# Where three weight scales are read, and where one scan sum is taken, in a fused attention and gated-GLU kernel

## The chip, the cores and the metric

One Trainium2 chip, one core. The time is the device time of one execution in microseconds; the median of three runs is given. A profile is one further execution, recorded by the hardware profiler, with a time of its own.

## The reference

Everything is bf16 outside, with x of 2048 rows and 640 columns. B is a gated unit with 1536 hidden features. A is attention with 32 heads of 192, in which every query sees the last 512 cached keys (Sk // 4 of 2048).

```python
xn = layernorm(x)
q = (xn @ wq) split into 32 heads of 192
k, v = k_cache[:, :, Sk - W:], v_cache[:, :, Sk - W:]        # W = 512
s = softmax(q @ k.T * 192 ** -0.5) @ v, heads joined, @ wo
g = silu((sigmoid(xn @ w_gate) * (xn @ w_up)) @ w_down)
out = x + s * g
```

## The kernel before

The work has three stages. The first (lines 404 to 541) normalizes x and computes the hidden features of B. The second, about 124 to 643 us, is attention in 16 runs. The third multiplies by wo and w_down and joins the parts. The order of all instructions is written out by hand: each engine takes its own in the order in which the program issues them, and waits in place where an operand is not ready.

**The runs.** A run r is a pair (pi, g): half pi of the queries (1024 rows), group g of four heads. Even runs have pi = 0, odd ones pi = 1, and g is r // 2. A run has a score phase of 16 steps, k = 0 to 15, and then a value phase of 8 products, k = 0 to 7.

- A step of the score phase is `stage_s` (six pairs of matmuls into a pair of PSUM banks, line 663, then one exp on ACT, line 667) and then `phase_s`, which issues whatever else belongs to that step. Banks 4 to 7 take turns, so the scores of step k wait for the exp of step k - 2.
- A product of the value phase is `stage_pv`: 16 matmuls (line 677), a reciprocal and a scaling on VectorE (lines 683 and 684), and after every second one a DMA transpose of the result on SP's queue (line 690). The transposed result is stored later, also by SP (`store_o`, line 697).

**Queries of the next run.** In the same score steps, eleven query slots compute the next run's queries (`query_slots`; `q_after` puts them at k = 1, 2, 3, 4, 5, two at 6, then 8, 10, 12, 14). They use seven products where eight would be plain, in a half-and-half scheme on fp16 sums of the weights. Their matmuls are line 569; VectorE copies a product out of PSUM (line 590) and adds it to another (line 607). The slots share banks 0 to 3 with the value products that follow: the second value product needs the banks that slot 10, at k = 14, frees with its last add.

**Scales.** The fp16 sums need weights scaled by a power of two. There is one scale for two groups, four in all, each from the absolute sums of five chunks of wq:

- `scan_load(i, buf)` loads chunk i by SP; `scan_abs(i)` (line 202) takes the absolute sum per partition on ACT. Chunks 5n to 5n + 4 belong to scale n. The tables `scans_s` and `scans_pv` say at which (r, k) of the score phase or of the value phase a sum is taken.
- `set_scan(n)` calls `set_scale`: VectorE takes the maximum of the five columns, cuts it to a power of two, spreads it over a tile mx_b, and SP transposes it by DMA into mx_row (line 213), so that each partition then holds all 128 values. Table `sets` gives the place.
- `set_scale2` reads the row: a maximum over mx_row (line 216), a product (line 217) and a reciprocal (line 218), all on VectorE. Table `sets2` gives the place. This is what "reading a scale" means here.

The first scale is set and read in the first stage. The other three are set at (1, 1), (4, 1) and (9, 1). Scale n serves groups 2n and 2n + 1: `weights(g, c)` scales raw weights with it on ACT in the value phases, two runs or so ahead, and `scale_k` (line 170) multiplies K with its inverse, at k = 12 of an even run (14 in run 2) and at k = 7 of an odd one. K comes into the tile kraw by two DMAs on SP (`load_k`, line 161), for an even run at k = 2 and at k = 12 or 14.

The places in `phase_s` that matter, in their order within a step:

```python
for j in q_after.get(k, ()) if q_list else ():
    q_list[j]()
...
if pi == 0 and g + 1 < NG:
    if k == 2:
        load_k((g + 1, 0))
    elif k == (14 if g == 1 else 12):
        scale_k((g + 1, 0))
        load_k((g + 1, 1))
...
if (r, k) in scans_s:
    scan_abs(scans_s[r, k])
...
if (r, k) in sets2:
    n = sets2[r, k]
    set_scale2(mx, w_ups[n], w_downs[n])
```

Of the kernel before, what the change touches and what calls it, by code (L numbers as in the profile page):

```python
# [17 lines left out]
def kernel(  # L18
# [177 lines left out]
    def scan_load(i, buf):  # L196
        scan_t[i] = buf[:, 0:NSC]
        n, c = divmod(i, NCD)
        nc.sync.dma_start(scan_t[i], wq_n[:, c, n * NSC:(n + 1) * NSC])
# [536 lines left out]
    for n, k in enumerate((0, 1, 7, 2, 3, 8, 4, 5, 9, 6, 10)):  # L736
# [5 lines left out]
        elif n == 4:  # L742
            for i in range(6):
                scan_load(NCD + i, scan_bufs[i])
    scans_s = {(0, 4): 10, (0, 10): 11}
    scans_pv = {(0, 0): 5, (0, 1): 6, (0, 2): 7, (0, 4): 8, (0, 6): 9, (1, 7): 12, (2, 7): 13, (3, 7): 14}
    scans_pv.update({(4 + n, 7): 15 + n for n in range(NCD)})
    scans_load = {(0, 6): (11, 5), (1, 4): (12, 4), (2, 4): (13, 5), (3, 4): (14, 4)}
    scans_load.update({(4 + n, 4): (15 + n, 5 - n % 2) for n in range(NCD)})
    sets = {(1, 1): 1, (4, 1): 2, (9, 1): 3}  # L750
    sets2 = {(1, 8): 1, (4, 9): 2, (9, 8): 3}
    scale_s = {0: 2, 3: 3, 15: 4}
    q_after = {1: (0,), 2: (1,), 3: (2,), 4: (3,), 5: (4,), 6: (5, 6), 8: (7,), 10: (8,), 12: (9,), 14: (10,)}

# [444 lines left out]
```

## Time and profile before

| | before |
|---|---|
| median of three runs | 877.39 us (876.77 to 877.61) |
| profiled execution, its own time | 877.93 us |
| its span | 876.1 us |
| TensorE busy | 865.4 us, 7557 matmuls |
| VectorE busy | 674.9 us |
| ACT busy | 628.5 us |
| GpSimd busy | 234.8 us |
| mean granted TensorE clock | 0.998 |

The span runs from the first to the last recorded instruction. An engine counts as busy while one of its instructions runs. The granted clock is the share of full speed that TensorE was given. A wait is put down to the instruction that ended last before the waiting one began. In the views below, PE is TensorE, DVE is VectorE, ACT is ScalarE, POOL is GpSimd and SP is the engine whose queue issues most DMAs.

### The profile page before, as it was taken

What the parts mean: (1) busy time and instruction counts of PE and PEld (TensorE: products, weight loads), DVE (VectorE), ACT (ScalarE), POOL (GpSimd) and SP (SyncE); (2) the same over time, 40 slices, a digit from 0 to 9 for tenths busy, and PEclk for the clock granted to TensorE, in tenths of its full rate; (3) what the DMA queues carried; (4) which work ended last, traced back from release to release, by engine and by line L of the source; (5) the groups of instructions that cost most, each with busy time, mean ns of one, the idle gap of its engine ahead of it and who ended that gap; (6) DMA issues with size and microseconds to landing.
All of it is one profiled execution on the core that took longest, in us unless ns stands there. A gap on an engine that the chain in (4) does not pass through costs nothing.

```text
span 876.1 us, 19052 instructions
## 1 busy us (share of the span) xinstructions
PE 865.4 (99%) x7557; PEld 570.9 (65%) x7557; DVE 674.9 (77%) x1148; ACT 628.5 (72%) x783; POOL 234.8 (27%) x320
## 2 busy tenths in 40 slices
PE   9999999999998999999999999999999999999998
PEld 5444446576676775775775775775777777777775
DVE  6586767877875776776877877888788788979997
ACT  4766568799797889889889688648556566866662
POOL 0085076062360443443442442300000111000000
PEclk9999999999999999999999999999999999999999
DMA  9895983978998899899989968899696977776641
GB/s 281 185 249 109 243 240 83 262 101 234 227 165 218 156 209 237 181 205 241 169 168 225 170 120 206 206 220 261 140 277 184 302 240 221 235 251 219 224 136 37
DMA packets 258873, 175.98 MB, mean 201 GB/s; under 512 B 162976, under 2 KB 241440, under 8 KB 258784
## 3 DMA queue, kind: packets, MB, share of 16 engines
q1 hardware_dynamic: 253248, 157.26, 72.4%
q0 software_dynamic: 5536, 17.50, 10.4%
q8 instruction: 59, 0.97, 0.5%
q14 instruction: 30, 0.25, 0.1%
HBM read 101.71 MB, written 36.70 MB: 158 GB/s over the span
## 4 chain that ended last, share of the span: by engine, by line
PE 94%; ACT 2%; DMA 1%; DVE 1%; SPq 1%; issue 0%; DVEq 0%; ACTq 0%
PE ps_all L1007 25%; PE ps_all L677 20%; PE ps_all L569 19%; PE ps_all L663 18%; PE ps_all L484 11%; ACT E L667 1%; PE ps_all L387 1%; ACT arm L722 1%; DMA mx_row<-mx_b 0%; DMA kraw<-in_A_k_cache_dram 0%; SPq L697 0%; DMA x_sb<-in_A_x_dram 0%; DVE arm L991 0%; DVE arm L1062 0%; DVE arm L1060 0%
## 5 line engine op out<-in xcount | busy, mean ns | idle before, releaser
L667 ACT ACTIVATE E<-ps_all 128x1024 bf16<-128x1024 f32 x256 | 251.6, 1024 | 97.9 <-PE ps_all L663 97.7
L663 PE MATMUL ps_all<-qT,kT 64*128 64x512 bf16 x1536 | 199.9, 378 | 0.9 <-ACT E L667 0.8
L677 PEld LDWEIGHTS <-E 128*128 128x128 bf16 x2048 | 169.7, 98 | 8.3 <-issue 8.3
L677 PE MATMUL ps_all<-v_sb,E 128*128 128x193 bf16 x2048 | 174.1, 247 | 0.1
L607 DVE TENSOR_TENSOR qT<-ps_all,qp 128x512 bf16<-128x512 f32 x174 | 115.6, 687 | 47.8 <-PE ps_all L569 38.3
L1007 PEld LDWEIGHTS <-mid 128*128 128x128 f16 x1236 | 120.3, 98 | 46.0
L663 PEld LDWEIGHTS <-kT 64*128 64x128 bf16 x1536 | 86.6, 94 | 79.6 <-issue 6.1
L590 DVE COPY qp<-ps_all 128x512 f32<-128x512 f32 x150 | 100.5, 687 | 43.8 <-PE ps_all L569 43.6
L684 DVE TENSOR_TENSOR o_st<-ps_all,rden 128x768 bf16<-128x768 f32 x128 | 122.5, 957 | 4.7 <-DVE rden L683 0.3
L569 PE MATMUL ps_all<-mid 64*128 64x512 f16 (+1 forms) x840 | 106.8, 377 | 3.5 <-DVE qp L590 3.5
L569 PE MATMUL ps_all<-mid,arm 64*128 64x512 f16 (+1 forms) x840 | 105.6, 376 | 0.0
L569 PEld LDWEIGHTS <-mid 64*128 64x128 f16 x840 | 50.3, 94 | 46.4 <-issue 5.5
L569 PEld LDWEIGHTS <-arm 64*128 64x128 f16 x840 | 47.1, 94 | 44.5 <-issue 0.5
L1007 PE MATMUL ps_all<-arm,mid 128*128 128x320 f16 x480 | 70.4, 299 | 0.0
L808 ACT ACTIVATE mid<-mid,w_sc 128x1536 f16<-128x1536 bf16 (+1 forms) x43 | 61.4, 1451 | 0.0
L240 ACT ACTIVATE mid<-mid,w_sc 128x1536 f16<-128x1536 bf16 x37 | 58.1, 1571 | 1.1 <-DVE w_sc L218 0.7
L1007 PE MATMUL ps_all<-op,mid 128*128 128x320 f16 (+1 forms) x408 | 58.1, 295 | 0.0
L490 DVE TENSOR_TENSOR hT_sb<-ps_all,sig_sb 128x512 bf16<-128x512 f32 x48 | 32.8, 686 | 28.3 <-PE ps_all L484 20.7
L489 ACT ACTIVATE sig_sb<-ps_all 128x512 bf16<-128x512 f32 x48 | 28.4, 596 | 35.3 <-PE ps_all L484 33.9
L258 POOL TENSOR_TENSOR arm<-mid 128x384 f16<-128x384 f16 x20 | 18.2, 909 | 119.9 <-ACT mid L240 118.9
L258 POOL TENSOR_TENSOR mid<-mid 128x384 f16<-128x384 f16 x20 | 18.2, 909 | 118.9 <-ACT mid L240 117.9
L1007 PE MATMUL ps_all<-mid 128*128 128x320 f16 x348 | 49.9, 299 | 0.0
(183 smaller groups left out, 1094.1 us busy)
## 6 DMA issues: line engine op xcount, KB each, us to landing
oT_d<-oT SPq DMA_DIRECT2D x64, 384.0 KB, 5.0
mid<-oT_d SPq DMA_DIRECT2D x46, 384.0 KB, 4.1
mid<-in_A_wq_dram POOLq DMA_DIRECT2D x64, 192.0 KB, 7.1
arm<-in_A_wo_dram SPq DMA_DIRECT2D x16, 480.0 KB, 6.3
h_d<-hT_sb SPq DMA_DIRECT2D x16, 384.0 KB, 4.5
kraw<-in_A_k_cache_dram SPq DMA_DIRECT2D x32, 192.0 KB, 3.4
v_sb<-in_A_v_cache_dram SPq DMA_DIRECT2D x32, 192.0 KB, 5.8
arm<-in_A_wq_dram SPq DMA_DIRECT2D x15, 384.0 KB, 4.7
```

The lines of the kernel that those rows point to most:

```text
L240: nc.scalar.activation(raw.bitcast(F16), raw, AF.Copy, scale=w_ups[g // 2])
L258: tt(TB, part_w(g, c, a, 1, 1), part_w(g, c, a, 0, 1), ALU.subtract)
L484: nc.tensor.matmul(gu[:, i, :], lhsT=w[:, c, f * P:(f + 1) * P], rhs=xnT[s][:, c, :], start=(c == 0), stop=(c == NCD - 1),)
L569: nc.tensor.matmul(ps_all[:, b, :], lhsT=w(r, c), rhs=x[r, c, :], start=(first and k == 0), stop=(k == len(cs) - 1), skip_group_check=True,)
L590: nc.vector.tensor_copy(dst, part(b))
L607: nc.vector.tensor_tensor(q_out(i, u, pp), part(b), t, ALU.add)
L663: nc.tensor.matmul(ps[:, b, :], lhsT=kT[h, c * PC + j, :], rhs=qT_t[r][i, j][h, pp, :], start=(j == 0), stop=(j == PC - 1),)
L667: nc.scalar.activation(E_t[r, i, pp][:, c, :, :], ps, AF.Exp, scale=scale_qk)
L677: nc.tensor.matmul(o_ps[:, q // 2, q % 2, 0:DH + 1], lhsT=E[:, c, h, q * P:(q + 1) * P], rhs=vt[:, c, 0:DH + 1], start=(c == 0), stop=(c = ...
L684: nc.vector.tensor_tensor(o_st[:, :, h * DH:(h + 1) * DH].rearrange("p (b i) d -> p b i d", b=2), o_ps[:, :, :, 0:DH], rden[:].to_broadcas ...
L808: eng.activation(t, t.bitcast(BF16), AF.Copy, scale=up)
L1007: nc.tensor.matmul(ps_all[:, b, d0:d1], lhsT=a[:, c, :], rhs=w[:, c, d0:d1], start=(start and c == 0), stop=(c == nk - 1), skip_group_chec ...
```

## The change

Three entries of `sets2` move: the read of scale 1 from step 8 to step 12 of run 1, that of scale 2 from step 9 of run 4 to step 0 of run 5, that of scale 3 from step 8 to step 12 of run 9. The places of `set_scan` stay. The absolute sum of chunk 11 moves from step 10 of run 0 to the end of its value phase, behind the last product. The load of that chunk stays at step 6. No instruction is added or taken away, and the orders on TensorE, GpSimd and SP stay as they are.

```diff
-    scans_s = {(0, 4): 10, (0, 10): 11}
-    scans_pv = {(0, 0): 5, (0, 1): 6, (0, 2): 7, (0, 4): 8, (0, 6): 9, (1, 7): 12, (2, 7): 13, (3, 7): 14}
+    scans_s = {(0, 4): 10}
+    scans_pv = {(0, 0): 5, (0, 1): 6, (0, 2): 7, (0, 4): 8, (0, 6): 9, (0, 7): 11, (1, 7): 12, (2, 7): 13, (3, 7): 14}
     scans_pv.update({(4 + n, 7): 15 + n for n in range(NCD)})
     scans_load = {(0, 6): (11, 5), (1, 4): (12, 4), (2, 4): (13, 5), (3, 4): (14, 4)}
...
     sets = {(1, 1): 1, (4, 1): 2, (9, 1): 3}
-    sets2 = {(1, 8): 1, (4, 9): 2, (9, 8): 3}
+    sets2 = {(1, 12): 1, (5, 0): 2, (9, 12): 3}
```

## The prediction

> **What bounds the kernel now.** I read the busy shares first, then PE's waits, then the 16 attention runs one against another, then each odd run's chain and queues.
>
> ```profile
> PE 865.4 (99%) x7557; PEld 570.9 (65%) x7557; DVE 674.9 (77%) x1148; ACT 628.5 (72%) x783; POOL 234.8 (27%) x320
> PE ps_all L569 <- DVE qp L590: 3.5, 1, 3.5
> PE ps_all L663 <- ACT E L667: 0.8, 1, 0.8
> ```
>
> The first line is the page's busy time, the other two are from PE's waits (total, times, longest). TensorE works 99% of the 876.1 us, so only what stops or slows it counts. Two stops lie in the part that the diff touches: one of 3.5 us behind a VectorE copy, one of 0.8 us behind an exp.
>
> Next I cut the runs at their first score matmul and asked for busy time by stretch. Columns: the stretch, its length, then each engine's busy time, granted clock, DMA share, GB/s.
>
> ```profile
> 124.14:157.93 33.79, 32.90 (x331) 22.53 (x328) 26.42 (x43) 26.79 (x32) 21.90 (x31) 1.00 0.58 128
> 157.93:190.61 32.68, 32.68 (x332) 20.52 (x333) 25.07 (x47) 28.44 (x36) 7.60 (x10) 1.00 0.83 200
> ...
> 256.04:294.18 38.14, 34.65 (x331) 26.14 (x333) 25.54 (x47) 29.67 (x33) 15.85 (x21) 0.96 0.80 167
> 294.18:326.89 32.71, 32.71 (x332) 21.90 (x333) 24.07 (x40) 28.43 (x36) 10.55 (x14) 1.00 1.03 210
> 326.89:359.82 32.93, 32.87 (x332) 21.98 (x333) 24.33 (x40) 29.55 (x33) 16.02 (x22) 1.00 0.92 208
> ```
>
> These are runs 0, 1, 4, 5 and 6. An undisturbed run takes 32.71 us. Run 4 takes 38.14 (5.43 too many), run 0 takes 33.79 (1.08 too many), run 6 takes 32.93 (0.22 too many). Run 1, which holds a scale read too, loses nothing; nor does run 9 (32.71).
>
> **Run 4.** From the chain of waits there (start, length, what):
>
> ```profile
> 270.12 2.09 SPq L697
> ...
> 272.27 4.29 DMA mx_row<-mx_b
> ...
> 276.58 0.30 DVE w_sc L216
> ...
> 277.25 0.60 DVE qp L590
> 277.86 0.04 issue
> 277.90 1.26 PE ps_all L569 x10
> ```
>
> VectorE had the row ready for its transpose at about 261, but SP's queue stood in the stores of line 697 and issued the transposing DMA at 272.27. The read at step 9 stands in front of a copy (line 590) that TensorE needs, so all wait until 276.56. By the starts of equal matmuls, run 6 goes on 18.10 us after its beginning, run 4 at 277.90 - 256.04 = 21.86: 3.76 us lost. Then TensorE is slow (one-microsecond stretches of PE: length, busy, clock, DMA share, GB/s):
>
> ```profile
> 277.90:278.90 1.00, 1.00 (x10) 1.00 0.02 6
> 278.90:279.90 1.00, 1.00 (x10) 0.60 0.00 0
> 279.90:280.90 1.00, 1.00 (x8) 0.50 0.00 0
> 280.90:281.90 1.00, 1.00 (x8) 0.50 0.00 0
> 281.90:282.90 1.00, 1.00 (x10) 0.70 0.53 155
> ```
>
> Lost to the clock: 0.40 + 0.50 + 0.50 + 0.30 = 1.70 us. 3.76 + 1.70 = 5.46, the 5.43 of the run.
>
> **Part 1: the read of run 4 moves to step 0 of run 5.** The stall goes, as the row has landed some 12 us before the new place. What is late next? In the same run at step 12 VectorE scales K from kraw, whose loads stand on SP right behind the transpose (SP issues them from 273.63). Today the stall hides that. Without it VectorE is there as in run 6, which shows this wait:
>
> ```profile
> 344.21 4.23 DMA kraw<-in_A_k_cache_dram
> ...
> 348.46 0.42 DVE k_sb L170
> ```
>
> Run 6's second half of kraw landed at 348.44, which is 21.55 us into the run; the late scaling pushed back the last query add (end at 350.29), for which the second value product waited: 0.22 us. For run 4, SP's semaphore row on the same load line ends its wait at 277.6, and the landing times of this window are at most 3.4 us after issues at 273.63 and about 274.2; so kraw is there at 277.6, 21.56 us into the run. That is run 6 to a hundredth. I take run 6's loss, 0.22. Bounds: nothing, if it lands 0.3 us sooner; above, the slowest landing of line 161 in the traced runs, 5.9 us (run 2), would make it 280.1, so 2.5 us more, at one microsecond of TensorE for each. Run 4: 38.14 - 32.93 = 5.21 saved.
>
> At its new place the read takes 0.78 us of VectorE (run 1's own: from 174.13 to the next copy at 174.91). In run 4's own first step VectorE idles 1.33 us before the first copy, and run 5 begins alike: cost 0. It issues no DMA; SP's and POOL's orders stay. Its readers (weight scaling in run 5's value phase, K in run 6) come 15 us later or more.
>
> **Part 2: the reads of runs 1 and 9 go from step 8 to step 12.** Neither waits today (transposes issued at 164.04 and 436.63, landed 5.0 and 2.9 us later, read at 174.13 and 441.47), so nothing is gained. Queued behind the new place is the copy of step 14 and its add, on which the second value product waits. In run 1 the adds ahead end at 178.64; with 0.78 the copy starts at 179.42 instead of 179.02, and its add ends 1.49 later at 180.91, 22.98 us into the run. Run 6's product was ready at 350.11, 23.22 us in. So 0.2 us of cover is left: cost 0, and if the cover were gone, 0.4 in each at most.
>
> **Part 3: the scan sum.** In run 0, ACT (start, length, what):
>
> ```profile
> 141.59 1.50 ACT L202 ACTIVATE arm<-arm 128x1536 bf16<-128x1536 bf16 x1
> 142.97 0.21 ACT L202 ACTIVATION_READ_ACCUMULATOR arm<-arm 128x1 f32 x1
> 143.06 3.88 ACT L667 ACTIVATE E<-ps_all 128x1024 bf16<-128x1024 f32 x4
> ```
>
> One absolute sum, 1.47 us to the next instruction, stands before four exps back to back, and the scores of two steps wait: 0.80 and 0.26 us of TensorE, 1.06 of the run's 1.08. Run 6 has the same steps without the sum and loses nothing there. At the new place, behind the last value product's entry in ACT's order, five sums end at 155.55 and the next exp waits for TensorE until 158.78: 3.23 us idle, of which a sixth takes 1.47 to 1.66. Its load was issued at 133.17, and its result is wanted only in run 4. Gain 1.08, bounds 0.80 (the named wait alone) and 1.11 (by the value phases' starts).
>
> **The sum.** The profiled execution took 877.93, with 1.83 outside the span of 876.1. Span: 876.1 - 5.21 - 1.08 = 869.8; that execution would take 871.64. The median of the three runs is 0.54 below it, so 877.39 - 6.29 = **871.1 us**. About 0.2%, 1.75 us, is what a measurement can tell here.
>
> [...] The row: 3.49 us without a matmul, then clock 0.50 to 0.60 for some 3 us. [...]
>
> **The rivals.**
>
> Slow clock only in the profiled execution. The gap is the same in every execution but its slow stretch may not be. Then the timed runs gain 3.76 - 0.22 + 1.08 = 4.62: 872.8. For it: the profiled time is above all three. Against: it is only 0.32 above the slowest, not 1.7. Chance 0.12. [...]
>
> A K load that comes later than I read. With the 5.9 us landing run 4 gives back 2.5 more: 873.6. For it: DMA share is 0.9 to 1.1 before the wait. Against: all DMAs up to 277 are issued as before. Chance 0.08.
>
> Slower: the stall is only passed on. Place: SP's queue in run 4. If its pause lets SP catch up, run 6's kraw would land 5.21 late, and TensorE would lose that plus 1.70 for the clock: 6.91 against 6.29, and with the 1.47 of a sum that still held back exps, 879.5. It decides from a slip of about 4.6 us. For it: SP issued run 4's transpose 11 us after it was ready. Against: in run 6 SP has issued all and waits from 345.7 to 348.9 although runs 5 and 6 had no pause, and run 8 repeats without loss (32.71). Chance 0.04.
>
> That the edit does nothing is out: the order of VectorE's instructions does move, and the 3.5 us name that read.
>
> **How the numbers follow.** Forecast 0.76, the rest as above. Low end: no kraw loss (870.9) less the runs' scatter of 0.6 and the 0.03 of part 3's upper bound: 870.2. High end: 873.6, the late K load, which takes in the clock rival. Below and above lie the slower case and part of the scatter. Faster by over 0.2%: 0.76 + 0.12 + 0.08, less 0.01 for what I have not seen, 0.95; slower 0.04; same 0.01.
>
> **What would show it.** Right: no PE wait on line 590; no DVE wait on mx_row after the first; run 4 at 32.9 us with clock 1.00 and a kraw wait of some 0.3; run 0 at 32.7; runs 1, 5 and 9 as before. Wrong: a kraw wait of over 1 us in run 4, a PE wait in the second value product of runs 1 or 9, a first exp of run 1 that waits for ACT, or a longer run 6.

## The result, and the profile after

The changed kernel takes 871.51 us (median of six runs, 871.22 to 872.36) against 877.08 us (875.24 to 877.77) for the kernel before in the same comparison: a ratio of 0.9941, interval 0.9928 to 0.9954. The forecast was 871.1, with a range from 870.2 to 873.6. The profiled execution took 872.36 with a span of 870.2, the slowest of the six; the other five have spans of 869.3 to 869.9.

The page's busy time:

```profile
PE 863.0 (99%) x7557; PEld 570.7 (66%) x7557; DVE 674.5 (78%) x1148; ACT 628.5 (72%) x783; POOL 234.3 (27%) x320
```

PE's waits (what waited for what: total, times, longest):

```profile
PE ps_all L377 <- DVE warm L371: 1.3, 1, 1.3
PE ps_all L677 <- DVE qT L607: 0.8, 1, 0.8
PE ps_all L387 <- ACT mid L402: 0.7, 2, 0.5
```

The wait of 3.5 us on a copy (line 590) and that of 0.8 us on an exp are gone. The first and the last line lie ahead of the attention runs. A new wait is there: a value product waits 0.8 us for the last query add. Runs 0, 4, 5, 6 and 8, each cut at its first score matmul (stretch, length, busy times, clock, DMA share, GB/s):

```profile
123.64:156.51 32.87, 32.87 (x334) 22.94 (x332) 26.55 (x44) 27.12 (x33) 22.02 (x32) 1.00 0.59 125
...
254.61:288.40 33.79, 32.94 (x331) 26.13 (x333) 25.02 (x44) 29.55 (x33) 16.74 (x23) 1.00 0.93 194
288.40:321.11 32.71, 32.71 (x331) 21.91 (x333) 24.56 (x43) 28.43 (x36) 9.60 (x14) 1.00 0.95 209
321.11:353.82 32.71, 32.71 (x331) 21.89 (x333) 24.16 (x40) 29.55 (x33) 15.79 (x22) 1.00 0.83 199
386.53:419.44 32.91, 32.88 (x331) 21.91 (x333) 24.34 (x40) 29.56 (x33) 15.98 (x22) 1.00 0.93 200
```

Run 4 fell from 38.14 to 33.79 and its clock from 0.96 went to 1.00. Run 0, which is 34.08 in the kernel before by this cut, is 32.87. Run 6 no longer loses its 0.22, and run 8 now loses 0.20. Run 4 is not at the 32.93 that was forecast, and its chain of waits says why:

```profile
272.30 0.97 SPq L213
...
273.94 3.05 DMA kraw<-in_A_k_cache_dram
...
277.02 0.42 DVE k_sb L170
277.44 0.61 DVE qp L590
...
278.15 0.70 DVE qT L607
...
278.89 9.49 PE ps_all L677 x112
```

This is the wait that the forecast named as next: K waits for kraw, behind it the copy, the add and then the second value product. Here and below, a time into run 4 is counted from its first score matmul in the timeline, 254.53 in this profile and 255.97 in the one before. In this execution SP issued the loads at 273.33, 18.8 us into the run (17.7 in the profile before), so VectorE waited 1.19 us and TensorE 0.85, as the last figures of these two rows of the timeline say:

```profile
276.52 0.93 DVE L170 TENSOR_SCALAR k_sb<-kraw,w_sc 128x768 bf16<-128x768 bf16 x2 [1.19 <-DMA kraw<-in_A_k_cache_dram]
...
278.89 9.49 PE L677 MATMUL ps_all<-v_sb,E 128*128 128x193 bf16 x112 [0.85 <-DVE qT L607]
```

### The profile page after: what moved, and what is told of

It is laid out like the page before. It is cut to its first block, busy times and chain, and to the rows that moved or that the text cites. A ratio compares the mean times of both kernels' runs of the same rounds, so it can differ in the third digit from the quotient of the medians.

```text
span 870.2 us, 19053 instructions
## 1 busy us (share of the span) xinstructions
PE 863.0 (99%) x7557; PEld 570.7 (66%) x7557; DVE 674.5 (78%) x1148; ACT 628.5 (72%) x783; POOL 234.3 (27%) x320
## 4 chain that ended last, share of the span: by engine, by line
PE 97%; DVE 1%; DMA 1%; SPq 0%; issue 0%; ACT 0%; DVEq 0%
PE ps_all L1007 26%; PE ps_all L569 21%; PE ps_all L677 20%; PE ps_all L663 19%; PE ps_all L484 11%; PE ps_all L387 1%; DMA kraw<-in_A_k_cache_dram 0%; DVE stats L349 0%; DVE arm L991 0%; DMA x_sb<-in_A_x_dram 0%; DVE arm L1062 0%; DVE arm L1060 0%; DVE qp L590 0%; DVE xn L364 0%; SPq L213 0%
## 5 line engine op out<-in xcount | busy, mean ns | idle before, releaser
L489 ACT ACTIVATE sig_sb<-ps_all 128x512 bf16<-128x512 f32 x48 | 28.4, 596 | 35.3 <-PE ps_all L484 33.8
```

## The experiments

Each was compared with the kernel before, run beside it. The medians of that kernel were 877.26, 877.77, 877.26 and 877.99 us for experiments 1 to 4, 5 to 8, 9, and 10 and 11.

### 1. The read of run 4 alone

```diff
-    sets2 = {(1, 8): 1, (4, 9): 2, (9, 8): 3}
+    sets2 = {(1, 8): 1, (5, 0): 2, (9, 8): 3}
```

> Only the read of scale 2 moves, from step 9 of run 4 to step 0 of run 5; scan sum 11 and the other two reads stay as before. The changed kernel's trace shows run 0 shorter by 1.21 us, but run 4 at 33.79 instead of the forecast 32.93, with a kraw wait of 1.19 us. Theory A (SP's queue in run 4 goes by its own schedule of transposes and stores, not by run 4's beginning): with run 0 as long as before, run 4 begins 1.4 us later, kraw lands as soon after its beginning as in the kernel before, and run 4 takes 32.9 to 33.0. The time is then the changed kernel's within about 0.3 us: 871.5 to 871.9. Rival B (run 4's kraw wait has nothing to do with when run 4 begins, and the parts add): run 4 stays at 33.8, run 0 at 33.8 to 34.1, and the time is 871.5 + 1.2 = 872.7.

872.55 us (872.29 to 872.95), ratio 0.9933, interval 0.9908 to 0.9957. Run 4:

```profile
256.13:288.91 32.78, 32.78 (x331) 25.71 (x333) 25.04 (x44) 29.55 (x33) 15.82 (x22) 1.00 0.93 195
```

The time speaks for B (parts add). Run 4's 32.78 lies just below A's 32.9 to 33.0 and a microsecond below B's 33.8. SP issued the kraw loads 17.2 us into the run here, and no wait for them is left.

### 2. The scan sum alone

```diff
-    scans_s = {(0, 4): 10, (0, 10): 11}
-    scans_pv = {(0, 0): 5, ..., (0, 6): 9, (1, 7): 12, ...}
+    scans_s = {(0, 4): 10}
+    scans_pv = {(0, 0): 5, ..., (0, 6): 9, (0, 7): 11, (1, 7): 12, ...}
```

> Only scan sum 11 moves to the value phase of run 0; all three reads stay as before. Theory A: run 0 is 1.1 to 1.2 us shorter, but the transpose that run 4's read waits for lands at nearly the same absolute time (0.3 us sooner), so the stall of run 4 grows from 3.5 to about 4.4 us: run 4 takes 39.0 and the time falls by only 0.3, to 876.8. Rival B (parts add): run 4 stays at 38.15, and the time falls by 1.1 to 1.2, to 875.9.

876.10 us (874.53 to 876.80), ratio 0.9976, interval 0.9959 to 0.9993: 1.16 us saved between the medians, within B's 1.1 to 1.2 (the interval allows 0.6 to 3.6). The run 0 of its profile is 32.86. Theory A falls: the stall of PE on line 590 did not grow to 4.4 us but is 2.9. Run 4 is 35.88, which neither theory had: the stall is 0.6 us shorter than in the kernel before, and the slow clock did not come (the gap, then one microsecond each, PE alone):

```profile
273.00:276.00 3.00, 0.18 (x2) 1.00 0.68 230
276.00:277.00 1.00, 1.00 (x12) 1.00 0.00 0
277.00:278.00 1.00, 1.00 (x14) 1.00 0.00 0
```

Its twelve runs fall into two groups: three of 874.53 to 875.06 with a mean granted clock of 1.000, and nine of 876.00 to 876.80 with 0.998. A stall of this kind costs about 1.5 us more where the clock falls, and it does not fall every time.

### 3. The reads of runs 1 and 9 alone

```diff
-    sets2 = {(1, 8): 1, (4, 9): 2, (9, 8): 3}
+    sets2 = {(1, 12): 1, (4, 9): 2, (9, 12): 3}
```

> Only the reads of scales 1 and 3 move, from step 8 to step 12 of runs 1 and 9. Theory A and the prediction: no change, 877.1 within 0.5; runs 1 and 9 at 32.7, the copy of step 14 begins up to 0.4 us later and nothing waits for it. Rival C (the cover of 0.2 us in the second value product is gone): runs 1 and 9 each 0.2 to 0.4 us longer and a PE wait of line 677 on line 607 in both, 877.6 to 877.9.

877.12 us (874.96 to 881.50), ratio 0.9992, interval 0.9972 to 1.0011: no difference. Runs 1 and 9 take 32.68 and 32.71, and no value product waits. Its run 4 shows the other face of the stall: PE's wait on line 590 is 2.8 us, shorter than in experiment 2, and yet the clock falls:

```profile
275.00:277.70 2.70, 0.43 (x5) 1.00 0.76 254
277.70:278.70 1.00, 1.00 (x8) 0.50 0.00 0
278.70:279.70 1.00, 1.00 (x8) 0.50 0.00 0
279.70:280.70 1.00, 1.00 (x7) 0.50 0.00 0
```

### 4. The changed kernel, with the K load ahead of the transpose on SP

```diff
-    sets = {(1, 1): 1, (4, 1): 2, (9, 1): 3}
+    sets = {(1, 1): 1, (4, 3): 2, (9, 1): 3}
```

> The changed kernel with scale 2 set at step 3 of run 4 instead of step 1, so that SP issues the two kraw loads of step 2 ahead of the transposing DMA; the read stays at step 0 of run 5. Theory A (kraw is late because it stands behind SP's queue, of which the transpose is 1.4 us): kraw is issued at about 271.9 instead of 273.3, lands 1.1 to 1.4 us sooner, the kraw wait of run 4 falls from 1.19 to below 0.2 and run 4 from 33.79 to 32.7 or 32.8: 870.5. Rival D (kraw is late because the DMA engines are full, whatever stands ahead on SP): kraw is issued sooner but lands as before, run 4 stays at 33.5 to 33.8 and the time at 871.5.

871.68 us (871.13 to 871.95), ratio 0.9920, interval 0.9892 to 0.9948. The profile does what A says, the loads issued 14.5 us into the run and run 4 at 32.71 with no kraw wait; its span is 869.5. SP's queue there (start, length, what):

```profile
269.60 2.63 SPq L161 DMA_DIRECT2D kraw<-in_A_k_cache_dram  x2
272.33 1.14 SPq L213 DMA_TRANSPOSE mx_row<-mx_b  x1
```

But the median misses A's 870.5 and is not below the changed kernel's. That fits a loss in run 4 that most executions of the changed kernel do not have, as experiment 10 shows of one.

### 5. The changed kernel, with run 4's K scaling at step 14

```diff
-            elif k == (14 if g == 1 else 12):
+            elif k == (14 if g in (1, 2) else 12):
```

> The changed kernel with run 4's first K scaling (and the load behind it) at step 14 instead of 12, as run 2 has it. In the changed kernel's profile this scaling waited 1.19 us for kraw ahead of the copy of step 14, and run 4 took 33.79; in the runs so far the load was issued between 15.8 and 18.8 us after run 4's beginning, in executions that share everything up to there. Theory A' (the loss in run 4 is that wait, and its size is the scatter of SP's queue): the scaling now follows the last query add, no PE wait of line 677 on line 607 is left in run 4, and run 4 takes 32.7 whatever the load does; 871.2 to 871.6, and the slowest executions (872.4 in the changed kernel) are gone. Rival B' (a scaling that ends late delays the value phase's VectorE work all the same): run 4 stays at 33.2 to 33.8 in an execution with a late load.

871.31 us (871.13 to 871.80), ratio 0.9925, interval 0.9913 to 0.9937. Run 4 is 32.77. As forecast by A'; but this execution issued the loads early (16.2 us into the run), so its profile cannot show that a late load would be covered.

### 6. The kernel before, with the read one step later

```diff
-    sets2 = {(1, 8): 1, (4, 9): 2, (9, 8): 3}
+    sets2 = {(1, 8): 1, (4, 10): 2, (9, 8): 3}
```

> The kernel before, with the read of scale 2 one step later, at step 10 of run 4 instead of 9; all else as before. The read then stands behind the copy of step 10 and ahead of the adds of step 12, for which TensorE waits only at step 14. Theory A' (the loss is the idle time that reaches TensorE, and the half clock comes by chance after idle times of about 3 us): TensorE idles 2.0 us or less, the clock stays at 1.00, and run 4 takes 34.2 to 34.9 instead of 37.4 to 38.2: 873.0 to 874.0, with a smaller scatter than before. Rival C' (any stop of TensorE of a microsecond or two brings the half clock): run 4 takes 36 to 36.6, 875 to 876.

874.05 us (872.59 to 876.36), ratio 0.9958, interval 0.9944 to 0.9972. The read still waited, for 1.8 us:

```profile
275.58 0.29 DVE L216 TENSOR_REDUCE w_sc<-mx_row 128x1 f32<-128x128 bf16 x1 [1.77 <-DMA mx_row<-mx_b]
```

Run 4 took 33.02 in the profile, less than either theory said, since the row landed early there; the median lies just over A's band. One step takes back more than half of the loss, because the copy of step 10 now goes ahead of the read. That the scatter would shrink was wrong: it is 3.8 us, as in the kernel before beside it.

### 7. The kernel before, with the read at step 12

```diff
-    sets2 = {(1, 8): 1, (4, 9): 2, (9, 8): 3}
+    sets2 = {(1, 8): 1, (4, 12): 2, (9, 8): 3}
```

> The kernel before, with the read of scale 2 at step 12 of run 4, right behind the K scaling; all else as before. The row lands at 20.5 us into the run or so, ahead of kraw at 21.6. Theory A' (it is the place in VectorE's order that costs, not the read): the read waits for nothing, adds its own 0.78 us behind the K scaling and ahead of the copy that the second value product needs: run 4 takes 33.4 to 34.0 and the time is 873.0 to 873.3, some 0.6 us over the kernel that moves it to run 5 (872.55). Rival D' (the 0.78 us has cover there, as in runs 1 and 9): run 4 takes 32.8 to 33.0, 872.5.

873.06 us (872.75 to 875.34), ratio 0.9948, interval 0.9935 to 0.9961. The read waits for nothing. The time is A's; run 4 in the profile, 32.90 with 0.2 us of waiting, is D's. The kernel before beside it was 0.5 us slower than beside experiment 1 too, so whether the read's own VectorE time costs anything there is left open.

### 8. The transpose issued by ACT

```diff
-    sets = {(1, 1): 1, (4, 1): 2, (9, 1): 3}
+    sets = {(1, 1): 1, (4, 5): 2, (9, 1): 3}
...
-        nc.sync.dma_start_transpose(mx_row[:], mx_b[:])
+        eng.dma_start_transpose(mx_row[:], mx_b[:])      # eng = nc.scalar for scale 2
```

> The kernel before, its read of scale 2 still at step 9 of run 4, but the transposing DMA is issued by ACT's queue, and scale 2 is set at step 5 instead of 1, where ACT has some slack. Theory A' (the row is late because it stands behind the stores on SP's queue): issued at about 12 us into the run instead of 16.3, the row lands at about 15.5, before the read at 16.1; the stall of line 216 falls from 4.4 to below 1 us and TensorE's from 3.5 to below 0.5, less some 1 us that ACT's exps lose to the issue; 872.5 to 873.5. Rival E' (the DMA engines are full, so the row lands late from any queue): the row lands over 5 us after its issue, and the stall stays above 2 us: 875 or more.

881.57 us (879.64 to 882.58), ratio 1.0040, interval 1.0026 to 1.0055: slower, and for neither reason. ACT's part of the timeline, and the matmul that waited:

```profile
271.18 1.40 ACTq L213 DMA_TRANSPOSE mx_row<-mx_b  x1
272.63 1.94 ACT L667 ACTIVATE E<-ps_all 128x1024 bf16<-128x1024 f32 x2 [5.08 <-issue]
...
273.70 1.46 PE L663 MATMUL ps_all<-qT,kT 64*128 64x512 bf16 x6 [5.01 <-ACT E L667]
```

On ACT the built program waits for seven DMA semaphores ahead of the instruction, in four rows of the trace of 17 ns to 6.73 us. The longest of those rows begins at 264.26 and takes 6.73 us, and the exps stood behind it. It ends as a V load that SP had issued at 265.25, on one of that row's two semaphores, lands at 270.96. TensorE idled 5.0 us. No run here shows what happens without these waits, and why the program has the long one, for a load of V, is open. Why the row is late on SP stayed open for the next experiment.

### 9. The kernel before, with the row first on SP

Scale 2 is set at the end of run 3, ahead of the V loads and two stores; it is still read at step 9 of run 4.

```diff
-    sets = {(1, 1): 1, (4, 1): 2, (9, 1): 3}
+    sets = {(1, 1): 1, (9, 1): 3}
...
+        if r == 3:
+            set_scan(2)
         if pi == 1 and g + 1 < NG:
             for pp in range(G):
                 load_v(g + 1, pp, nc.sync)
```

> The kernel before, its read of scale 2 still at step 9 of run 4, but scale 2 is set at the end of run 3, so that on SP's queue the transposing DMA goes ahead of the four loads of V and the two stores that it stood behind, instead of after them. Theory A' (the row is late because of what stands ahead of it on SP): it is issued at about 265.8 instead of 272.3, lands at 269 to 270.5, before the read at 272.2; no DVE wait on the row, no PE wait on line 590, clock 1.00, run 4 at 32.7 to 33.2, and the time within 0.4 us of the kernel that moves only the read (872.55), although the read has not moved. Rival E' (the DMA engines are full, so a row takes as long as it takes from wherever it is issued): the row lands over 6 us after its issue, the stall of line 216 stays above 1 us, and the time is 874 or more.

872.52 us (872.08 to 872.81), ratio 0.9945, interval 0.9931 to 0.9959. SP's and VectorE's rows in the timeline, and then run 4:

```profile
263.53 1.31 SPq L213 DMA_TRANSPOSE mx_row<-mx_b  x1
...
271.95 0.28 DVE L216 TENSOR_REDUCE w_sc<-mx_row 128x1 f32<-128x128 bf16 x1
```

```profile
255.93:288.65 32.72, 32.72 (x331) 21.98 (x333) 25.31 (x47) 29.55 (x33) 15.81 (x22) 1.00 0.90 197
```

The row took 5.9 us to land, longer than the 4.3 of before, and was there 2.5 us ahead of the read. The stall came from SP's order: with the read left where it was, the time is that of experiment 1 to 0.03 us.

### 10 and 11. The changed kernel once more, and with both mends of the K load

Experiment 11 has the edits of 4 and 5 together.

> The changed kernel once more, as the measure for the run beside it. Theory A' (the wait for kraw in run 4 is there only in some executions): a median of 871.3 to 871.8 again, and a run 4 between 32.7 and 33.8 in the profile. Rival (the wait is there in every execution): run 4 at 33.5 or more again.

> The changed kernel with both: scale 2 set at step 3 of run 4, so that the kraw loads go ahead of the transpose on SP, and run 4's first K scaling at step 14. Theory A': run 4 takes 32.7 in every execution; the median falls by at most 0.4 us against the changed kernel beside it, to 871.1 to 871.4, and its slowest execution lies below 872. Rival (the changed kernel loses the 1.07 us of its profile in most executions): 0.8 to 1.1 us below it.

871.62 us (871.55 to 871.82; ratio 0.9924, interval 0.9911 to 0.9938) and 871.48 us (871.11 to 872.09; ratio 0.9923, interval 0.9909 to 0.9936). Run 4 of the two:

```profile
254.87:287.67 32.80, 32.80 (x331) 26.52 (x333) 25.12 (x44) 29.57 (x33) 15.86 (x21) 1.00 0.95 199
```

```profile
254.60:287.32 32.72, 32.72 (x331) 21.97 (x333) 24.75 (x44) 29.56 (x33) 15.85 (x21) 1.00 0.92 197
```

In the repeated changed kernel run 4 lost next to nothing, as A' of experiment 10 allows, while run 8 lost 0.45 to a kraw wait of 0.6 us. Experiment 11 lies 0.14 below it, near A' and far from its rival; that no execution would lie above 872 was wrong (872.09). No version tried is measurably faster than the changed kernel.

## Why the prediction was right, point by point

**Run 4's stall.** Right in place and cause. Experiment 1 moves the one read and takes 4.7 us, experiment 9 leaves the read and moves the row's DMA and takes the same. The forecast had 5.21 for it, from one execution. What was not right is that the 1.70 us of slow clock belong to every execution of the kernel before. Experiments 2 and 3 show gaps of nearly the same length without and with it, and the two groups of experiment 2's runs put it at some 1.5 us in nine of twelve. So the first rival was wrong as it was put (the slow clock was not in the profiled execution alone), but it is each execution that decides: of the 24 runs of the kernel before beside experiments 1 to 4, the five fastest (874.85 to 876.10) have a mean clock of 0.999 or 1.000, the rest 0.998 or less.

The traces show where the clock changed. Their record of the granted clock for the kernel before has 273.07 us at full clock, from 6.02 on, then 3.413 us at half, then 593.92 at full: the two long stretches are 80 and 174 times 3.4133 us. The changed kernel's record has 863.57 us at full clock, from 4.93 on, which is 253 times; experiment 3's has 273.07 us at full and then 3.41 at half; experiment 2's has 866.99 at full from 4.96 on, 254 times; experiment 8's, with an idle time of 5.0 us, has 6.83 at half, twice 3.41. A window here is a stretch of 3.4133 us, counted from where such a record begins. In these records the clock changed only at the ends of windows, and not at a fixed time behind the gap: half clock began 1.19 us after TensorE went on in the kernel before, 0.42 us after it in experiment 3. These are the windows around the gap (stretch, length, PE's busy time, clock, DMA share, GB/s), of the kernel before, experiment 3 and experiment 2:

```profile
275.68:279.09 3.41, 1.19 (x12) 1.00 0.62 201
279.09:282.50 3.41, 3.41 (x20) 0.50 0.06 13
...
274.28:277.69 3.41, 0.64 (x7) 1.00 0.91 232
277.69:281.10 3.41, 3.41 (x18) 0.50 0.00 0
...
271.20:274.61 3.41, 1.68 (x16) 1.00 1.10 221
274.61:278.03 3.42, 2.21 (x22) 1.00 0.37 138
```

In the first two most of the gap lies in one window, and the clock is half for the whole next one, although TensorE worked 1.19 and 0.64 us of the 3.41 in the window ahead of it. In experiment 2 a window's end cuts the gap in two, and the clock stays full. Where the gap begins in a window differs between executions: 0.22 us into one in experiment 3, 1.68 us into one in experiment 2.

**What is late next.** The K load, as said. Its size of 0.22 was read from one execution, and one sign that the forecast had set for being wrong, a kraw wait of over 1 us in run 4, came up in the profiled execution (1.19). In the nine profiles whose order on SP is the same up to there, SP issued the loads between 15.4 us (experiment 6) and 18.8 us (the changed kernel's profile) into run 4. Where neither the read nor another place of the scaling hides it, no such wait shows in experiments 1 and 10 (run 4 at 32.78 and 32.80), and it makes run 4 1.08 us longer in the changed kernel's profile. I had taken the landing time, 21.56 us into the run, as fixed. The bound of 2.5 us held. That the other five executions of the result were 0.5 to 1.1 us faster than the profiled one, most of them probably without this wait, is luck as far as the forecast goes. The same wait costs 0.2 to 0.6 us in run 6 or run 8 in six of the thirteen profiles, with the change and without it. My first explanation after the result, that SP goes by its own schedule whatever run 4's beginning, was refuted by experiment 2: its run 4 begins when the changed kernel's does, and SP issues the loads 3.1 us sooner.

**The scan sum.** Right in cause, and a little too small: the forecast was 1.08 with an upper bound of 1.11, run 0 fell by 1.21 in the profile, and experiment 2 gives 1.16. The forecast had cut run 0 at 124.14, 0.36 us after its first score matmul (123.78), which made the run 33.79 instead of 34.08. All six profiles that take the sum late have run 0 at 32.86 or 32.87, and all seven that take it early at 34.08. The sixth sum at the end of the value phase costs nothing, as this ACT view of the changed kernel shows:

```profile
155.39 0.19 ACT L202 ACTIVATION_READ_ACCUMULATOR arm<-arm 128x1 f32 x1
157.34 1.02 ACT L667 ACTIVATE E<-ps_all 128x1024 bf16<-128x1024 f32 x1 [1.76 <-issue]
```

Of the 3.23 us of idle time 1.76 are left.

**Runs 1 and 9.** No cost, as said (experiment 3), and with more cover than I had worked out. In the changed kernel's run 1 the read and the gap to the copy take 0.58 us (177.12 to 177.70), not 0.78, and VectorE still idles 0.71 us before the first product's result:

```profile
177.12 0.27 DVE L216 TENSOR_REDUCE w_sc<-mx_row 128x1 f32<-128x128 bf16 x1
...
177.70 0.67 DVE L590 COPY qp<-ps_all 128x512 f32<-128x512 f32 x1
178.47 0.69 DVE L607 TENSOR_TENSOR qT<-ps_all,qp 128x512 bf16<-128x512 f32 x1
179.87 0.18 DVE L683 RECIPROCAL rden<-ps_all 128x4 f32<-128x4 f32 x1 [0.71 <-PE ps_all L677]
```

**The slower rival.** Not seen: run 6 takes 32.71, less than before, where the rival had kraw 5.21 us late.

**The sum.** The span was forecast at 869.8 and five of six runs have 869.3 to 869.9. The time came out 0.4 above the forecast, and the term at fault is the last one: I took the 0.54 us by which the median lay below the profiled execution over to the changed kernel. Without that term the sum is 871.64. The saving itself was forecast at 6.29; it is 5.57 beside the kernel before's 877.08 of the result, and 6.37 beside its 877.99 of experiment 10. That difference is the kernel before's, most likely by how many of its executions had the slow clock, so how near the forecast time came is in part luck.

## What to carry to other kernels

A read that waits for a DMA costs what stands behind it on its engine: look on the reader's side for a later place with nothing urgent behind it, and on the queue's side for what stands ahead of the DMA; here either mend alone was worth the same 4.7 us. When a stall of the bound engine goes, name the next operand on the same queue and treat its landing time as a spread over executions (here its issue alone lay between 15.4 and 18.8 us into the run), not as the one number that a profile shows. Side work in an engine's stream belongs where that engine idles: 1.47 us of it between exps cost 1.16, behind the last value product nothing.

## What the runs showed of the hardware that was not expected

TensorE's clock went to half at the end of a window of 3.41 us in which it had worked 0.64 us (experiment 3) or 1.19 us (the kernel before), and stayed there for 3.41 us. It did not where a window's end cut a gap of 2.9 us so that 1.68 and 2.21 us of work were left in the two windows (experiment 2). So of two waits of nearly one length the shorter, 2.8 us, was followed by half clock and the longer, 2.9 us, was not; what follows a window with between 1.19 and 1.68 us of work, these runs do not show.

The transposing DMA that was put on ACT's queue stood behind semaphore waits, the longest of 6.73 us, and held the exps behind it (experiment 8). These waits are in the built program; they are not shown to be something that the chip asks for.
